# Sparse attention and GELU feed-forward: Winograd's seven products moved from the last batch's input product to unit 1's output product

## The chip, the cores and the metric

The kernel runs on one core of a Trainium2 chip. The time is device microseconds of one execution. Before the change the median of three runs is 221.82 us (221.53 to 222.54). The profiled execution has a span of 220.1 us from its first to its last instruction.

## What is computed

Local attention (window 16) together with block-summary attention, then a two-layer feed-forward with a GELU by sigmoid between the layers. There are 4 batches, 8 heads, 768 positions and a head size of 64, so 3072 tokens of width 512; the hidden width is 2048.

```python
k_sum = k.reshape(B, H, nb, block, D).max(axis=3)       # block = 32, nb = 24
v_sum = v.reshape(B, H, nb, block, D).mean(axis=3)
scores_l = scale * np.matmul(q, k.transpose(0, 1, 3, 2))
scores_s = scale * np.einsum('bhsd,bhnd->bhsn', q, k_sum) + np.log(block)
scores_l_m = np.where(np.abs(pos[:, None] - pos[None, :]) < window, scores_l, -1e9)
a = softmax(np.concatenate([scores_l_m, scores_s], axis=-1))
x = np.matmul(a, np.concatenate([v, v_sum], axis=2))    # to tokens x 512
h = x @ w_in                                            # input product, 512 -> 2048
g = h * (1.0 / (1.0 + np.exp(-1.702 * h)))
out = g @ w_out                                         # output product, 2048 -> 512
```

## The kernel before, in words

Work goes by *units*: a unit is half a batch, 384 tokens (`HALF`), so there are units 0 to 7. For each unit the attention output is turned into `xT` (features on partitions, in two tiles of f16 per unit parity). The input product makes `gT` of 16 tiles of 128 hidden features, the *ff tiles*: each is four matmuls of 384 columns into a PSUM bank (`ph`), and ScalarE (ACT) writes the GELU of it to `gT`. The output product takes 128 tokens at a time, an *output tile*; a unit has three. Plainly done (`ff_out`, line 788) an output tile is 16 matmuls of 512 columns into one bank (`po`), in four parts of four.

Units 2 to 7 form their output tiles in pairs by Winograd's form of Strassen's method (class `Pair`): the product of two output tiles is cut into quarters, and seven products of half size, `p1` to `p7`, each of eight matmuls of 256 columns, give all four quarters of both tiles. The sums of the left factors are made on VectorE (DVE) by `sums`, those of the weights once by `w_sums`; between products parts of the result are copied out of PSUM by ACT (`held`) or added by DVE.

Every operation goes through a helper that records it (`_Ordered`, line 28), so the order on each engine is the order in which the Python code calls, and nearly all instructions have line 28 in the profile. Groups are told apart by the names of their tiles.

The stages that the change touches:

- Unit 1's output product is the loop at the end of `for u in range(2)` (line 1067 on). It has 12 slots (three tiles by four parts). After each slot `beside` puts in work for batch 1's attention, by the table `plan1` (line 1038): `t` turns a pair of heads of q on TensorE (PE) and copies it, `s` and `S` are `scores` (12 matmuls for a half of a pair of heads, an exponential on ACT, a multiplication with the mask on DVE), `v` is `values` (24 matmuls, then a reciprocal and a multiplication on DVE for each of two pairs), `x` turns the result into `xT`. Two pools of PSUM serve all this: `pmm`, four tiles of one bank, and `psb`, two tiles of two banks each. Scores and turned q use `psb`; in this stage `values` uses `pmm`, two tiles at a time. `w_sums(3)` comes after slot 2, and the transposes of batch 2's keys by DMA (`xk`, on the SP queue) after slot 3.
- The units 2 to 5 run through a common loop (line 1176): `ff_in` for each ff tile of one unit, then of the next, with other work put between. After it come the three pairs' 21 products in the order of line 1110.
- The last batch (units 6 and 7) takes another way, `ff_in_pairs` (line 704). Eight ff tiles of unit 6 are made plainly. Then DVE forms the first sums for the pairs of output tiles (`early`) and four sums `xsum` of the two units' `xT`. After that, for four pairs of ff tiles of both units together, seven products of two matmuls each (`A`, `Bp`, `C`, `Dp`) stand in place of eight; unit 7's eight plain ff tiles (`one(u + 1, ...)`) are put between. The sums `wsum` of the input weights are made on DVE in the batch before (`win_weights`, line 691). Between the products DVE moves a partial result from one PSUM tile to another (`px_in`, `pw_in`) or adds a held one (`m`, `c`), and ACT copies or does the GELU.

The order inside a pair of ff tiles is this:

```python
def A(i):
    prod(x, wt[0, 0], b11, i, True)
    dve.tensor_copy(out=y, in_=x)
    prod(v, ws[2], t[2], i, True)
    copy(act, hold[i], v)
def Bp(i):
    prod(x, ws[1], t[1], i)
    dve.tensor_add(v, x, hold[i])
    prod(y, wt[0, 1], b21, i)
    gelu(u, f0(i), y)
```

Of the kernel before, what the change touches and what calls it, by code (L numbers as in the profile page):

```python
# [9 lines left out]
F32 = mybir.dt.float32  # L10
# [25 lines left out]
def kernel(  # L36
# [648 lines left out]
            for nt in range(N0):  # L685
                act.activation(out=gT[0][:, nt, :], in_=ph0[nt], func=ACT.Gelu_apprx_sigmoid)

    WI = 4
    wt = {}

    def win_weights(i0, i1):

        if i0 == 0:
            w = w_in_sb.rearrange("p k (i e c) -> p e k i c", e=2, c=128)[:, :, :, NI - WI:]
            wt.update({(e, h): w[:, e, 2 * h:2 * h + 2] for e in range(2) for h in range(2)})
            wt["s"] = stage.tile([128, 4, 2, WI, 128], F16, name="wsum", tag="kf")
        o, i = [wt["s"][:, n, :, i0:i1] for n in range(4)], slice(i0, i1)
        a11, a12, a21, a22 = (wt[e, h][:, :, i] for e in range(2) for h in range(2))
        dve.tensor_add(o[0], a21, a22)
        dve.tensor_sub(o[1], o[0], a11)  # L700
        dve.tensor_sub(o[2], a11, a21)
        dve.tensor_sub(o[3], a12, o[1])

    def ff_in_pairs(u, early):

        (b11, b21), (b12, b22) = xTT
        xs = castp2.tile([128, 4, 2, HALF], F16, name="xsum", tag="kb")
        t = [xs[:, n] for n in range(4)]
        big = [psb.tile([128, 1024], F32, name="pw_in", tag="big") for _ in range(2)]
        mm = [pmm.tile([128, 512], F32, name="px_in", tag="mm") for _ in range(4)]  # L710
        X = [big[0][:, 0:HALF], big[1][:, 0:HALF], mm[0][:, 0:HALF]]
        V = [b[:, 512:512 + HALF] for b in big]
        Y = [m[:, 0:HALF] for m in mm[1:3]]
        L = mm[3][:, 0:HALF]

        def gelu(w, f, src):
            act.activation(out=gT[w % 2][:, f, :], in_=src, func=ACT.Gelu_apprx_sigmoid)

        def one(w, f, ps):
            for ko in range(KO):  # L720
                pe.matmul(out=ps, lhsT=w_in_sb[:, ko, f * 128:(f + 1) * 128], rhs=xT[w % 2][ko],
                          start=(ko == 0), stop=(ko == KO - 1))
            gelu(w, f, ps)

        def prod(ps, a, b, i, first=False):
            for k in range(2):
                pe.matmul(out=ps, lhsT=a[:, k, i], rhs=b[:, k], start=(first and k == 0),
                          stop=(k == 1), skip_group_check=True)

        ws = [wt["s"][:, n] for n in range(4)]  # L730
        hold = {}

        def A(i):
            x, v, y = X[i % 3], V[i % 2], Y[i % 2]
            prod(x, wt[0, 0], b11, i, True)
            dve.tensor_copy(out=y, in_=x)
            prod(v, ws[2], t[2], i, True)
            hold[i] = attp.tile([128, HALF], F32, name="m7", tag="x2")
            copy(act, hold[i], v)

        def Bp(i):
            x, v, y = X[i % 3], V[i % 2], Y[i % 2]
            prod(x, ws[1], t[1], i)
            dve.tensor_add(v, x, hold[i])
            prod(y, wt[0, 1], b21, i)
            gelu(u, f0(i), y)

        def C(i):
            x, v = X[i % 3], V[i % 2]
            prod(x, ws[0], t[0], i)  # L750
            c = attp.tile([128, HALF], F32, name="c22", tag="a_sb")
            dve.tensor_add(c, x, hold[i])
            prod(v, wt[1, 1], t[3], i)
            gelu(u, f0(i) + 1, v)
            gelu(u + 1, f0(i) + 1, c)

        def Dp(i):
            x = X[i % 3]
            prod(x, ws[3], b22, i)
            gelu(u + 1, f0(i), x)  # L760

        def f0(i):
            return 2 * (NI - WI + i)

        free = [X[0], X[1], X[2], V[0], V[1], Y[0], Y[1], L]
        for f in range(2 * (NI - WI)):
            one(u, f, free[f % 8])
        early()
        for n, (x, y) in ((2, (b22, b12)), (0, (b12, b11)), (1, (b22, t[0])), (3, (b21, t[1]))):
            dve.tensor_sub(t[n], x, y)  # L770
        rest = list(range(2 * (NI - WI)))
        for i in range(WI + 1):
            if i < WI:
                A(i)
            if i:
                C(i - 1)
            one(u + 1, rest.pop(0), L)
            if i < WI:
                Bp(i)
            if i:  # L780
                Dp(i - 1)
            if i < WI - 1:
                one(u + 1, rest.pop(0), L)
        assert not rest

    po_now = {}

    def ff_out(u, ms, part):
# [38 lines left out]
    def bank(name):  # L827
        return pmm.tile([128, d_model], F32, name=name, tag="mm")
# [6 lines left out]
    class Pair:  # L835
# [51 lines left out]
            self.w = bank("pw")  # L887
            product(self.w, self.a21, ts["t3"], True)

        def p2(self):  # L890
            y = bank("py")
            product(y, self.a12, ts["b21"], True)
            dve.tensor_add(self.osb(0)[:, 0:DH], y[:, 0:DH], self.t1)
            self.store(0, 0, False)

        def p4(self):
# [133 lines left out]
    for p in range(NP):  # L1030
# [5 lines left out]


    plan1 = {0: ["t0"], 1: ["t1"], 2: ["s0", "s1"], 4: ["t2"], 5: ["t3"],
             6: ["v0", "s2", "s3"], 8: ["x0"], 9: ["v1", "S0", "S1"], 11: ["x1", "S2", "S3"]}

    plan0 = {-1: ["q0", "q1", "q2", "q3", "s0", "s1"], 3: ["v0", "s2"], 5: ["x0", "s3"], 7: ["v1"], 9: ["x1"]}

# [2 lines left out]
    def beside(u, slot):  # L1045
        b, half = u // 2, u % 2
        for what in (plan0 if u == 1 else plan1).get(slot, ()):
            i = int(what[1])
            if what[0] == "t":
                tq1(i, dve if i % 2 else act)  # L1050
            elif what[0] == "q":
                q_turn(i, 1)
                q_copy(i, dve, 1)
            elif what[0] == "s":
                scores(b, half, i)
                if half and i == NP - 1:
                    gelu_soon()
            elif what[0] == "S":
                scores(b, 1, i)
                if i == NP - 1:  # L1060
                    gelu_soon()
            elif what[0] == "v":
                values(b, half, i, u == 1)
            else:
                tx(i, half)

    for u in range(2):
        todo = {}
        if u == 0:
            for p in range(NP):  # L1070
                todo.setdefault(12 + p // 2, []).append(lambda p=p: cast_q(dve, p, 1))
        else:
            def value_rows():
                vsum(1, range(NJ))
                block_sums()
                halo_dmas(w51, 0)
                sum_dmas(w51, 0)
                load_vc(2)
                load_qc(2)

            todo = {0: [lambda: tk(0, 1)], 3: [lambda: tk(1, 1)], 5: [lambda: v_odd(1)],
                    6: [lambda: tk(2, 1)], 9: [value_rows], 11: [lambda: tk(3, 1)]}
            ff_in(u, range(3))
        for nt in range(0 if u else N0, NT):
            if u == 0 or nt > 2:
                ff_in(u, (nt,))
            for f in todo.get(nt, ()):
                f()
        exp_soon()
        if u == 0:  # L1090
            beside(1, -1)
            load_qc(1)
            load_kc(2)
            busy(6)
        order = [(ms, part) for ms in range(JH) for part in range(4)]
        if u == 0:

            order = [(ms, part) for part in range(4) for ms in range(JH)]
        for i, (ms, part) in enumerate(order):
            ff_out(u, ms, part)  # L1100
            beside(u + 1, i)
            if u == 0 and i in (4, 7, 10):
                w_sums(i // 3 - 1)
            if u == 1 and i == 2:
                w_sums(3)
            if u == 1 and i == 3:
                for g in range(2):
                    xk(g, 2)

    order = ["a7", "a2", "a6", "b1", "a5", "b7", "a3", "a4", "b6", "b2", "b5",  # L1110
             "c1", "b3", "c7", "c6", "c2", "c5", "b4", "c3", "c4"]
# [16 lines left out]
    for b in range(1, B):  # L1128
# [17 lines left out]
        if more:  # L1146
# [21 lines left out]
            when = 7 if b == 1 else 14  # L1168
            first.setdefault(when, []).append(lambda: [xq(g, n) for g in range(2)])
            first.setdefault(9 if b == 1 else 15, []).append(bring)  # L1170
        if b == B - 2:
            for n0 in range(WI):
                first.setdefault(n0, []).append(lambda n0=n0: win_weights(n0, n0 + 1))
        if not more:
            ff_in_pairs(u, lambda: pairs["a"].sums(0, NI - WI))
        for w, todo in ((u, first), (u + 1, second)) if more else ():
            ff_in(w, range(3))
            for nt in range(NT):
                if nt > 2:
                    ff_in(w, (nt,))  # L1180
                for f in todo.get(nt, ()):
                    f()
        pairs["a"].p1(act)
        if more:
            exp_soon()
        if more:
            for m in "bc":
                pairs[m].sums(NI - 1, NI)
        else:
            pairs["a"].sums(NI - WI, NI)  # L1190
            for m in "bc":
                pairs[m].sums(0, NI)
        for what in order:
            getattr(pairs[what[0]], "p" + what[1])()
            if more:
# [32 lines left out]
```

## Time and profile before

| what | value |
|---|---|
| median of three runs | 221.82 us |
| profiled execution, its own time | 221.82 us |
| its span | 220.1 us |
| mean granted clock of TensorE | 0.974 |
| PE busy | 204.5 us, 93% |
| DVE busy | 145.8 us, 66% |
| ACT busy | 123.2 us, 56% |
| POOL busy | 94.6 us, 43% |

The page's times are from the span's start. The busy lines say how long an engine had an instruction in flight; the chain of work that ended last says which instruction each next one had to wait for, followed back from the end. In that chain PE has 69% of the span. PEclk is the share of TensorE's clock that was granted. Matmuls overlap, so the mean duration of one (326 ns for 384 columns) is longer than the time until the next one: in the chain of waits, where the pieces join end to end, 64 such matmuls take 10.53 us.

### The profile page before, as it was taken

How to read it: one execution, taken by the hardware profiler on the slowest of the kernel's cores; microseconds unless marked ns; L12 is line 12 of the kernel's file. 1: busy time of each engine (PE TensorE's matmuls, PEld its weight loads, DVE VectorE, ACT ScalarE, POOL GpSimd, SP SyncE). 2: the span in 40 equal slices, each digit the busy share in tenths (PEclk: the TensorE clock that was granted, in tenths of full speed). 3: DMA queues.
4: the chain of work that ended last, by engine and by line, in shares of the span. 5: the costliest groups of instructions: out<-in, count | busy, mean ns of one | idle time of the engine just before them, and what ended most of it. 6: DMA issues, size and time to landing. Idle time of an engine off the chain costs nothing.

```text
span 220.1 us, 5530 instructions
## 1 busy us (share of the span) xinstructions
PE 204.5 (93%) x2185; PEld 138.2 (63%) x2185; DVE 145.8 (66%) x417; ACT 123.2 (56%) x232; POOL 94.6 (43%) x173
## 2 busy tenths in 40 slices
PE   7869999999799999999999999999999747899994
PEld 2747565556365665667888755678887423558883
DVE  6696936687956769945777862899677143349532
ACT  2773777256475597778334676774437613783220
POOL 7879989799979800609993011020000000000000
PEclk9996999999999999999999999999999967999998
DMA  6999999999999999999999999950433300000223
GB/s 159 297 171 205 268 220 215 157 155 236 153 160 138 160 128 213 155 123 74 121 194 145 167 216 160 107 104 3 131 86 105 112 0 0 0 4 0 95 74 119
DMA packets 96610, 29.34 MB, mean 133 GB/s; under 512 B 84480, under 2 KB 93600, under 8 KB 96584
## 3 DMA queue, kind: packets, MB, share of 16 engines
q0 software_dynamic: 67920, 14.88, 75.9%
q1 hardware_dynamic: 28664, 14.11, 33.0%
q8 instruction: 17, 0.28, 0.5%
q14 instruction: 9, 0.07, 0.1%
HBM read 27.26 MB, written 6.29 MB: 152 GB/s over the span
## 4 chain that ended last, share of the span: by engine, by line
PE 69%; POOL 12%; DMA 7%; DVE 7%; SPq 2%; issue 2%; ACT 0%; DVEq 0%; POOLq 0%
PE ph L28 20%; PE px L28 14%; PE pw L28 8%; PE px_in L28 5%; PE pw_in L28 5%; PE po L28 5%; PE py L28 4%; DMA kb<-in_k_dram 3%; PE ps_s L28 3%; PE ps_av L28 3%; POOL mk L28 2%; POOL kb L28 2%; POOL qb L28 2%; DMA qf<-in_q_dram 2%; DMA qb<-in_q_dram 2%; SPq L28 2%
## 5 line engine op out<-in xcount | busy, mean ns | idle before, releaser
L28 PEld LDWEIGHTS <-w_in_sb 128*128 128x128 f16 x472 | 46.0, 99 | 32.9 <-issue 4.5
L28 PE MATMUL ph<-xT,w_in_sb 128*128 128x384 f16 x384 | 65.0, 326 | 0.0
L28 ACT ACTIVATE gT<-ph 128x384 f16<-128x384 f32 x96 | 45.6, 490 | 21.0 <-PE ph L28 20.8
L28 PEld LDWEIGHTS <-gT 128*128 128x128 f16 x384 | 35.6, 98 | 12.4
L28 ACT ACTIVATE a_sb<-ps_s 128x768 bf16<-128x768 f32 x28 | 21.2, 806 | 11.4 <-PE ps_s L28 11.4
L28 PE MATMUL po<-w_out_sb,gT 128*128 128x512 f16 x96 | 23.1, 380 | 0.0
L28 PEld LDWEIGHTS <-ss 128*128 128x128 f16 x216 | 21.0, 98 | 2.5
L28 DVE TENSOR_TENSOR a_sb<-a_sb,mk 128x768 bf16<-128x768 bf16 x28 | 15.5, 556 | 8.6 <-ACT a_sb L28 7.1
L28 ACT ACTIVATE t<-px 128x256 f32<-128x256 f32 x21 | 8.1, 384 | 20.0 <-PE px L28 20.0
L28 POOL DMA_DIRECT2D vw<-vw x12 | 6.6, 578 | 28.2 <-DVE vw L28 24.3
L28 PE MATMUL pw<-tb,gT 128*128 128x256 f16 x144 | 18.7, 273 | 0.0
L28 PE MATMUL px<-ta,ss 128*128 128x256 f16 x144 | 18.7, 273 | 0.0
L28 DVE TENSOR_TENSOR x<-ps_av,rc 128x384 f16<-128x384 f32 x28 | 15.6, 558 | 1.0
L28 POOL DMA_DIRECT2D vw<-in_v_dram x18 | 15.9, 936 | 0.2 <-issue 0.2
L28 DVE TENSOR_REDUCE ks<-kx 128x24 bf16<-128x768 bf16 x12 | 11.3, 943 | 6.0 <-DMA kx<-kb 6.0
L28 DVE TENSOR_TENSOR ss<-gT 128x512 f16<-128x512 f16 (+3 forms) x18 | 7.5, 418 | 9.9 <-ACT gT L28 9.9
L28 POOL DMA_DIRECT2D kb<-in_k_dram x16 | 13.2, 858 | 1.6 <-DMA w_out_sb<-in_moe_w_out_dram 1.2
L28 POOL DMA_DIRECT2D qb<-in_q_dram x16 | 13.3, 932 | 1.3 <-DMA vw<-in_v_dram 1.3
L28 ACT ACT_TABLE_LOAD x10 | 12.8, 1283 | 1.0 <-PEq L1212 0.8
L28 PE MATMUL px_in<-xT,w_in_sb 128*128 128x384 f16 x58 | 13.2, 360 | 0.0
L28 DVE TENSOR_TENSOR osb<-pw,t 128x256 f32<-128x256 f32 x18 | 7.6, 422 | 8.0 <-PE pw L28 4.8
L28 DVE RECIPROCAL rc<-ps_av 128x6 f32<-128x6 f32 x32 | 6.0, 188 | 7.1 <-PE ps_av L28 6.8
(126 smaller groups left out, 309.6 us busy)
## 6 DMA issues: line engine op xcount, KB each, us to landing
out_dram<-osb SPq DMA_DIRECT2D x18, 256.0 KB, 4.8
vw<-in_v_dram POOLq DMA_DIRECT2D x18, 128.0 KB, 5.5
w_in_sb<-in_moe_w_in_dram POOLq DMA_DIRECT2D x4, 512.0 KB, 8.6
w_out_sb<-in_moe_w_out_dram POOLq DMA_DIRECT2D x4, 512.0 KB, 16.0
kf<-in_k_dram SPq DMA_DIRECT2D x8, 192.0 KB, 4.2
kb<-in_k_dram POOLq DMA_DIRECT2D x16, 96.0 KB, 4.7
qb<-in_q_dram POOLq DMA_DIRECT2D x16, 96.0 KB, 7.0
out_dram<-osb SPq DMA_DIRECT2D x12, 128.0 KB, 1.7
```

The source lines that it names most:

```text
L28: r = f(*a, **kw)
```

## The change

Two edits. The first takes `win_weights` and `ff_in_pairs` out, and the last batch's units 6 and 7 go through the common loop of the other units. The sums of the three pairs are then placed as in batches 1 and 2.

The second replaces unit 1's twelve slots. Output tiles 0 and 1 become a `Pair`, tile 2 stays plain, and its four parts stand between the seven products. `p2` is split, so that the addition and the store of its result come later (`c11`). `w_sums(3)` is called ahead of the slots. In `plan1` `x0` goes from slot 8 to 7 and `v1`, `S0`, `S1` go from slot 9 to 8. `values` takes one `psb` tile for both of its pairs of heads, in place of two `pmm` tiles.

```diff
-        def p2(self):
-            y = bank("py")
-            product(y, self.a12, ts["b21"], True)
-            dve.tensor_add(self.osb(0)[:, 0:DH], y[:, 0:DH], self.t1)
+        def p2(self, early=False):
+            self.y = bank("py")
+            product(self.y, self.a12, ts["b21"], True)
+            if not early:
+                self.c11()
+
+        def c11(self):
+            dve.tensor_add(self.osb(0)[:, 0:DH], self.y[:, 0:DH], self.t1)
             self.store(0, 0, False)
...
-             6: ["v0", "s2", "s3"], 8: ["x0"], 9: ["v1", "S0", "S1"], 11: ["x1", "S2", "S3"]}
+             6: ["v0", "s2", "s3"], 7: ["x0"], 8: ["v1", "S0", "S1"], 11: ["x1", "S2", "S3"]}
...
-                values(b, half, i, u == 1)
+                values(b, half, i, True)
...
-        order = [(ms, part) for ms in range(JH) for part in range(4)]
         if u == 0:
-
-            order = [(ms, part) for part in range(4) for ms in range(JH)]
-        for i, (ms, part) in enumerate(order):
-            ff_out(u, ms, part)
-            beside(u + 1, i)
-            if u == 0 and i in (4, 7, 10):
-                w_sums(i // 3 - 1)
-            if u == 1 and i == 2:
-                w_sums(3)
-            if u == 1 and i == 3:
-                for g in range(2):
-                    xk(g, 2)
+            for i in range(12):
+                ff_out(0, i % JH, i // JH)
+                beside(1, i)
+                if i in (4, 7, 10):
+                    w_sums(i // 3 - 1)
+
+    ss = stage.tile([128, 2, NI, 128], F16, name="ss", tag="vf")
+    pair = Pair((1, 0), (1, 1), ss)
+    w_sums(3)
+    for i, step in enumerate(("p2", "p1", 0, 1, 2, "p7", "p6", "p5", None, "p3", "p4", 3)):
+        if step == "p2":
+            pair.p2(True)
+        elif step == "p1":
+            pair.p1(act)
+        elif step in (0, 1, 2, 3):
+            ff_out(1, 2, step)
+        elif step:
+            getattr(pair, step)()
+        beside(2, i)
+        if i == 1:
+            pair.sums(0, NI)
+            pair.c11()
+        if i == 3:
+            for g in range(2):
+                xk(g, 2)
...
-        if b == B - 2:
-            for n0 in range(WI):
-                first.setdefault(n0, []).append(lambda n0=n0: win_weights(n0, n0 + 1))
-        if not more:
-            ff_in_pairs(u, lambda: pairs["a"].sums(0, NI - WI))
-        for w, todo in ((u, first), (u + 1, second)) if more else ():
+        for w, todo in ((u, first), (u + 1, second)):
             ff_in(w, range(3))
...
-        if more:
-            for m in "bc":
-                pairs[m].sums(NI - 1, NI)
-        else:
-            pairs["a"].sums(NI - WI, NI)
-            for m in "bc":
-                pairs[m].sums(0, NI)
+        for m in "bc":
+            pairs[m].sums(NI - 1, NI)
```

## The prediction

> **What bounds the kernel now.** I read the chain of waits in order of time first, since it says which engine sets the end in each stage; then the busy time and granted clock by stretches; then the order of time on single engines where the chain has gaps. From 60.35 us on the chain is nearly all PE: unit 1's output product runs from 63.45 to 78.96, and from there every stage is PE work end to end, but for the last batch's input product.
>
> ```profile
> 63.45 0.86 PE po L28 x4
> 64.31 0.34 PE ps_t L28 x6
> ...
> 66.70 0.46 PE ps_s L28 x24
> 67.16 1.83 PE po L28 x8
> ...
> 101.41 0.87 PE px L28 x8
> 102.28 0.87 PE pw L28 x8
> ...
> 124.53 10.53 PE ph L28 x64
> 135.07 0.45 PE ps_vs L28 x24
> 135.52 10.51 PE ph L28 x64
> ```
>
> These are start, duration and piece. A part of `ff_out` costs 0.86 us, one of the seven half-size products 0.87 us, a pair of score pieces 0.46 us. Batch 2's input product, of both units and with nothing in its way, is 10.53 + 10.51 = 21.04 us.
>
> The same product in the last batch takes 29.34 us, from 169.15 to 198.49, with fewer matmuls. The busy times by stretches (stretch, length, then busy time of PE, PEld, DVE, ACT, POOL, the granted clock, DMA) say why:
>
> ```profile
> 124.53:146.02 21.49, 21.49 (x155) 12.83 (x153) 14.94 (x52) 14.77 (x31) 3.40 (x6) 1.00 1.22 159
> 169.15:198.49 29.34, 23.20 (x123) 12.49 (x121) 11.20 (x22) 15.73 (x35) 0.00 (x0) 0.88 0.11 32
> ...
> 174.49:178.91 4.42, 0.32 (x3) 0.09 (x1) 3.71 (x8) 0.49 (x1) 0.00 (x0) 0.88 0.00 0
> 178.91:181.00 2.09, 2.09 (x7) 1.01 (x7) 0.00 (x0) 0.49 (x1) 0.00 (x0) 0.50 0.00 0
> 181.00:183.55 2.55, 2.55 (x9) 1.22 (x8) 0.57 (x1) 0.98 (x2) 0.00 (x0) 0.50 0.00 0
> ...
> 188.42:190.69 2.27, 1.62 (x10) 0.88 (x9) 1.15 (x3) 1.56 (x4) 0.00 (x0) 1.00 0.00 0
> ```
>
> PE stands still for over 4 us, the clock falls to half, and stays there until about 183.6. What it waits for is in PE's own order of time, the idle time and its releaser in brackets:
>
> ```profile
> 178.91 0.80 PE L28 MATMUL pw_in<-xsum,wsum 128*128 128x384 f16 x2 [4.10 <-DVE px_in L28]
> ...
> 190.69 0.48 PE L28 MATMUL pw_in<-xsum,w_in_sb 128*128 128x384 f16 x2 [0.65 <-DVE c L28]
> ```
>
> **Edit 1, the last batch.** Removed: 4 pairs x 7 products x 2 = 56 matmuls; added: 4 x 16 = 64. So PE has 128 matmuls of 384 columns in place of 120, 8 more at 0.164 us (10.53 / 64), 1.3 us more work. Removed with them is all that made 120 matmuls (120 x 0.164 = 19.7 us) last 29.34, that is 9.6 us: the wait of 4.42 us for DVE (three sums for the output pairs, four `xsum`, then the copy to `px_in`, one after the other from 175.04 to 178.86); the half clock after it (16 matmuls from 178.91 to 184.2 take 5.3 us instead of 2.6, so 2.7); and the later waits for one DVE operation on a PSUM tile, 0.65 us each where the chain shows them in full, the remaining 2.5 us together. The common loop waits for nothing of the kind: batch 2 does it in 21.04 us, its GELU takes 0.49 us of ACT for every 0.65 us of PE, and the sums for the output pairs lie beside it on DVE. The last batch has less beside it (no key halos, no `ps_vs`). I take 29.34 - 21.04 = **8.3 us off**. For the range: if only the 4.42 us wait and its clock went, it would be 4.42 + 2.7 - 1.3 = 5.8 us; more than 8.3 is not there, as PE would have to beat batch 2.
>
> The 16 `wsum` operations on DVE (0.28 us each, 4.6 us from 125.3) go too, at no gain: PE ran end to end there. The tail is the same 21 products, 198.49 to the end, 21.6 us, without a stall then or now: its first product needs `gT` of unit 6 only, made 10 us earlier, and the 6 + 3 sums that DVE did beside it are mostly done before.
>
> **Edit 2, unit 1, work.** Removed: 8 parts at 0.86 = 6.88 us. Added: 7 products at 0.87 = 6.09 us. **0.8 us off**, as all of this stage is PE (15.51 busy of 15.51). The first product needs the last GELU of the odd ff tiles in its eighth matmul only, at 63.45 + 7 x 0.109 = 64.2, and ACT ends it at 63.97.
>
> **Edit 2, the DVE and ACT side.** DVE gets three sums of 0.69 us, one subtraction of 0.69 and three additions of 0.42 more, 4.0 us on 9.65 busy of 15.51. In order: `w_sums(3)` from 63.6 to 65.2, the copy of turned q to 66.6, the sums to 68.55. `p7`, which needs them, is PE's next but three: 63.45 + 2 x (0.87 + 0.34) + 0.86 + 0.46 + 1.83 + 0.34 = 69.4. So they are hidden by 0.8 us; without this cover `p7` would be late by what exceeds it. ACT swaps two copies of 0.60 for four of 0.38, 0.3 us more, on 9.73 of 15.51, hidden by the same idle time.
>
> **Edit 2, new waits.** `values` now takes a `psb` tile, of which there are two. In the changed program, as built, `v0` and `v1` have one of the two and `s2`, `s3`, `S0`, `S1` all have the other. So `s3` must wait until the exponential of `s2` has read it, and `S1` for that of `S0`. Before, each found the other tile free. The price comes from the pair s0, s1:
>
> ```profile
> 66.64 0.52 PE L28 MATMUL ps_s<-qT,kx 64*128 64x64 bf16 x24
> ...
> 67.03 1.51 ACT L28 ACTIVATE a_sb<-ps_s 128x768 bf16<-128x768 f32 x2 [0.84 <-PE ps_s L28]
> ...
> 67.87 1.26 DVE L28 TENSOR_TENSOR a_sb<-a_sb,mk 128x768 bf16<-128x768 bf16 x2 [1.43 <-ACT a_sb L28]
> ```
>
> By the chain the first 12 of the 24 end at 66.70 + 0.23 = 66.93; ACT starts 0.10 later, runs 0.81 (mean of the group `a_sb<-ps_s`), and a released PE starts 0.05 later (178.86 to 178.91 above). That is **0.96 us, twice**, with PE idle, and behind the waiting matmul stands all PE work. The lower bound is nothing; the upper takes ACT late by one copy of 0.38, 1.34 us each. There is a third: `v1` needs the mask product of `s3`, which comes 0.10 + 0.81 + 0.03 + 0.59 (half of two in 1.18) + 0.05 = 1.58 us after `s3`; between them lie `p5` (0.98 with its start after scores), `x0` (0.34) and half of `v1` (0.25), 1.57 in all, where two parts and more lay before. I take nothing; up to 0.7 if DVE is late by an addition and the reciprocal. Sum of edit 2: -0.8 + 1.92 = **1.1 us on**, between -0.8 and +2.6.
>
> A rule speaks against these short waits. The Trainium skill, TensorE: Matmul & The Clock Gate, "A second HAM failure mode: psum-queue depth-cycling", says that frequent small idles between matmul groups, from cycling through PSUM, can make the clock go to and fro between half and full. By it the 6 us of PE work from the first wait to the next stage could take 12, and the time would be about 220.6 us. This trace has the same kind of wait, 0.65 us before 190.69, and the granted clock around it is 1.00; only the 4.42 us wait was followed by 0.50. I go by the row, 214.6 us.
>
> **SP and POOL queues.** `xk`'s four transposes stood in the SP queue behind the store of unit 1's first tile, which waited for `osb` until 69.02, and began at 69.62. Now only unit 0's stores are ahead, so they begin when batch 2's keys have landed, near 56.2 + 5.5 = 61.7 us. They then run beside the block rows for `v0`, the transfers `vw<-vs`, issued at 62.37 and 63.46, which land after 3.6 us, at 67.1. `v0` comes at 71.4, so 4.3 us of delay cost nothing. If they took as long as the slowest transpose (10.0 us), they would land at 73.5 and `v0` wait 2.0 us. I take 0. Unit 1's stores end at about 80, ahead of `dx`, which follows in the queue at 83 as before.
>
> **The sum.** 220.1 - 8.3 + 1.1 = 212.9 us of span; the profiled execution's time is 1.72 us over its span and equals the median, so 214.6 us.
>
> **Rivals.** *The new waits do not show* (0.12): ACT or order hides them; then edit 2 gives -0.8 and the time is 212.7. For it: ACT has 5.8 us idle in the stage. Against it: nothing is placed between `s2` and `s3`. *Unit 1 costs more* (0.13): `v0` waits 2.0 us for its rows, or ACT and DVE are late everywhere; 216.1 to 216.6; one spell of half clock alone (2.7) would give 217.3. For it: DMA engines are full at 67 to 79. Against it: 4.3 us of slack. *The last batch recovers less* (0.05): the low clock there has another cause and stays; 21.04 / 0.85 = 24.8, 3.7 less to gain, or 218.3 us. Against it: batch 2 ran at 1.00. *Slower* (0.04): the block rows queue behind all four transposes. These took 9.53 us to issue and up to 10.0 to land, so 61.7 + 19.5 = 81.2, and `v0` would wait 9.8 us, with the half clock 2.7 more: 227.1 us. It makes the kernel slower from a wait of 5.6 us (214.6 + 5.6 + 2.7 = 222.9), that is rows landing after 77.0. Against it: every `vw` transfer in that stage landed within 6.4 us.
>
> **How the numbers follow.** The forecast, 213.8 to 215.8, has 0.65, and 0.01 is left for mishaps that add up to no change. The range goes down to 212.5 for the first rival and up to 217.4 for the second. This kernel's measurements can tell 0.5%, 1.1 us, from no change. Faster 0.95, same 0.01, slower 0.04.
>
> **What would show it.** The changed profile should have 128 `ph` matmuls of the last batch in 21 us with a clock of 1.00 and no `px_in`; PE waits of about 1 us for ACT `a_sb` ahead of `s3` and `S1`; and unit 2's first `ph` at about 80.1 instead of 78.96. A PE wait for `vw` or for `ss`, a clock under 1.00 in unit 1, or a last batch over 22 us would prove a step wrong.

## The result, and the profile after

| | median | runs |
|---|---|---|
| before | 221.58 us | 220.94 to 222.54, six runs |
| changed | 214.95 us | 213.57 to 215.95 in five runs, 223.28 in a sixth |

The ratio is 0.9685 (95% interval 0.9638 to 0.9733): the changed kernel is faster by 3.2%, some 7 us. Some executions are disturbed, here the one of 223.28 us; the ratios, here and below, leave such executions out, the medians and ranges of the experiments do not. The profiled execution of the changed kernel took 214.01 us, with a span of 212.3.

The busy times by stretches of the changed kernel, for unit 1's output product and for the last batch's input product (columns as before: stretch, length, PE, PEld, DVE, ACT, POOL, clock, DMA):

```profile
61.83:79.02 17.19, 15.36 (x253) 11.60 (x252) 13.31 (x33) 10.39 (x17) 11.06 (x14) 1.00 1.97 130
169.93:190.73 20.80, 20.80 (x130) 12.58 (x129) 5.85 (x14) 14.76 (x31) 0.00 (x0) 1.00 0.15 45
```

The second line is the gain: 20.80 us, all of it busy, clock 1.00, where 29.34 us stood with a clock of 0.88. The first line is the price: 17.19 us with 15.36 busy, where the kernel before had 15.51, all busy:

```profile
63.45:78.96 15.51, 15.51 (x229) 8.96 (x228) 9.65 (x24) 9.73 (x15) 12.50 (x15) 1.00 1.72 139
```

The chain of waits of the changed kernel shows what fills the rest of unit 1:

```profile
61.83 0.87 PE py L28 x8
...
68.94 0.87 PE px L28 x8
...
70.03 0.54 PE ps_av L28 x23
70.57 0.30 PE ps_s L28 x12
...
70.89 0.82 ACT a_sb L28
...
71.75 0.35 PE ps_s L28 x12
72.11 0.98 PE px L28 x8
...
73.98 0.30 PE ps_s L28 x12
...
74.30 0.82 ACT a_sb L28
...
75.16 0.35 PE ps_s L28 x12
75.52 0.98 PE px L28 x8
```

Twice ACT's exponential stands between two halves of scores, and the chain goes through it. From `s2` at 70.57 to the product at 72.11 are 1.54 us; the pair took 0.46 before. So each wait costs 1.08 us. PE's waits over the whole execution, by what they waited for (us in total, times, longest):

```profile
PE ps_s L28 <- ACT a_sb L28: 1.8, 2, 0.9
...
PE ph L28 <- DMA xT<-x: 0.7, 1, 0.7
```

The second line is new too, and lies in batch 2. No full wait for the rows of `v0` shows in this execution, but `v0`'s 24 matmuls stretch from 69.81 to 70.57, 0.76 us in place of 0.50. The two transfers of the rows were issued at 62.37 and 63.56 (62.37 and 63.46 before), but landed only at about 69.7 and 69.9, just when `v0` began. The queues show what had changed: the order of time of the SP queue (start, duration, operation) and the rows' transfers (number, size of each, median us from issue to landing). The kernel before:

```profile
69.62 9.53 SPq L28 DMA_TRANSPOSE kx<-kq  x4
```

```profile
vw<-vs POOLq DMA_DIRECT2D x2, 148.5 KB, 3.6
```

The changed kernel:

```profile
61.22 8.75 SPq L28 DMA_TRANSPOSE kx<-kq  x4
```

```profile
vw<-vs POOLq DMA_DIRECT2D x2, 148.5 KB, 6.8
```

The transposes of batch 2's keys began 8.4 us earlier by the clock of the span and now run beside the rows `vw<-vs`, which landed 6.8 us after their issue in place of 3.6. An experiment below moves these transposes alone.

The span's account: last batch 8.54 off; unit 1 1.68 on (17.19 - 15.51); the new wait for `xT` 0.7 on; and unit 1 began at 61.83 instead of 63.45, 1.6 us earlier. That last part is not the change: in the profiled execution before, PE stood 1.59 us for DVE `ks` at 60.35, ahead of all that was edited. In no other profile is this wait longer than 0.2 us, and `before_filled` below, which has the same code up to there, began unit 1 at 61.7. -8.5 + 1.7 + 0.7 - 1.6 = -7.7, and the spans differ by 7.8. Without the earlier start the change is worth 6.2 us in these two profiles.

### The profile page after: what moved, and what is told of

Read it like the earlier page. It is cut to its first block, busy times and chain, and to the rows that moved or that the text cites. A ratio compares the mean times of both kernels' runs of the same rounds, so it can differ in the third digit from the quotient of the medians.

```text
span 212.3 us, 5559 instructions
## 1 busy us (share of the span) xinstructions
PE 201.9 (95%) x2217; PEld 140.9 (66%) x2217; DVE 136.7 (64%) x401; ACT 122.7 (58%) x230; POOL 94.8 (45%) x173
## 2 busy tenths in 40 slices
DMA packets 96610, 29.34 MB, mean 138 GB/s; under 512 B 84480, under 2 KB 93600, under 8 KB 96584
## 4 chain that ended last, share of the span: by engine, by line
PE 84%; DMA 10%; DVE 1%; POOL 1%; ACT 1%; SPq 1%; issue 0%
PE ph L28 39%; PE px L28 16%; PE pw L28 7%; PE po L28 7%; PE ps_av L28 4%; DMA xT<-x 4%; PE py L28 4%; DMA vb<-in_v_dram 4%; PE ps_s L28 3%; DMA kf<-in_k_dram 2%; PE ps_t L28 1%; PE ps_x L28 1%; POOL vb L28 1%; ACT a_sb L28 1%; DVE qT L28 1%; PE ps_vs L28 1%
## 5 line engine op out<-in xcount | busy, mean ns | idle before, releaser
L28 PE MATMUL ph<-xT,w_in_sb 128*128 128x384 f16 x512 | 86.0, 326 | 0.7 <-DMA xT<-x 0.7
L28 ACT ACTIVATE gT<-ph 128x384 f16<-128x384 f32 x128 | 60.9, 490 | 26.2 <-PE ph L28 26.0
L28 PEld LDWEIGHTS <-w_in_sb 128*128 128x128 f16 x512 | 49.4, 98 | 33.0 <-issue 1.2
L28 PEld LDWEIGHTS <-ss 128*128 128x128 f16 x240 | 23.1, 98 | 2.9
L28 DVE TENSOR_TENSOR ss<-gT 128x512 f16<-128x512 f16 (+3 forms) x22 | 8.7, 394 | 19.6 <-ACT gT L28 19.6
L28 PE MATMUL pw<-tb,gT 128*128 128x256 f16 x160 | 20.8, 273 | 0.0
L28 PE MATMUL px<-ta,ss 128*128 128x256 f16 x160 | 20.8, 273 | 0.0
L28 PE MATMUL po<-w_out_sb,gT 128*128 128x512 f16 x64 | 15.2, 380 | 0.0
L28 PE MATMUL ps_s<-qT,kx 64*128 64x64 bf16 (+3 forms) x400 | 10.0, 192 | 2.8 <-ACT a_sb L28 1.8
L28 PEld LDWEIGHTS <-kx 64*128 64x128 bf16 x400 | 7.7, 96 | 6.5 <-issue 5.9
```

What stands on the lines that cost most here:

```text
L28: r = f(*a, **kw)
```

## The experiments

Ratios are to the kernel before, run on the same chip as the kernel in question (its medians there: 220.8, 220.4, 220.5 and 220.9 us); in brackets stand 95% intervals.

**The two edits apart.** The first kernel, `last_plain`, is the kernel before with edit 1 only (`win_weights` and `ff_in_pairs` out, the common loop for the last batch); the second, `unit1_pair`, has edit 2 only.

> Edit 1 alone: the last batch goes through the common loop, unit 1 stays as before. My theory says that the whole gain is here: the last batch's input product falls from 29.3 to about 20.8 us, clock 1.00, and the time is 221.6 - 8.4 = 213.2 us, under the changed kernel's 214.95. Rival: unit 1's pair brings part of the gain (it has 0.8 us less PE work); then this alone gives more than 214.95.

> Edit 2 alone: unit 1 by the seven products, the last batch as before. My theory: slower by what the changed profile shows, unit 1 17.2 us instead of 15.5, that is 221.6 + 1.7 = 223.3 us, with two PE waits for the exponential of 0.9 us each. Rival, that the pair pays as its 0.8 us less PE work says: 220.8 us.

Measured: 212.79 us (211.90 to 213.58), ratio 0.9641 [0.9602, 0.9681]; and 224.15 us, ratio 1.0116 [1.0063, 1.0168]. By the ratios edit 1 alone gives 7.9 us and all of the gain; edit 2 alone costs 2.6 us (1.4 to 3.7). With both, the ratio is 0.9685, so beside edit 1 the second edit costs about 1 us (0.9685 / 0.9641 = 1.0046, across chips), though the two intervals overlap. The chain of waits of the kernel with edit 1 alone has a wait of its own:

```profile
79.37 2.59 PE ph L28 x16
81.96 8.17 DMA xT<-x
...
90.18 1.95 PE ph L28 x11
```

Unit 1 is 1.6 us shorter there, and PE stands 0.7 us at 90.18 for unit 3's `xT`. What a slower unit 1 loses, this wait can give back in part. But the changed kernel's wait of 0.7 us in batch 2 is not in this kernel, so by the two profiles the waits cancel and do not explain why the cost is nearer to 1 us than to 1.7.

**The half clock.** `before_filled` is the kernel before, with four plain ff tiles of unit 7 ahead of the sums that PE waited for; they no longer stand between the half-size products. The matmuls are the same.

```diff
+        rest = list(range(2 * (NI - WI)))
+        for n in range(4):
+            one(u + 1, rest.pop(0), free[n])
         early()
...
```

> The kernel before, with four of unit 7's plain ff tiles moved ahead of the first sums, so that PE has 2.6 us more to do while DVE makes them. My theory of the last batch: the wait of 4.1 us falls to about 1.7, which is too short to halve the clock, so 2.4 + 2.7 = 5.1 us are won; the DVE waits further on have less work beside them and give 0.5 to 1.5 us back: 216.5 to 217.5 us, clock 1.00 throughout. Rival, that the half clock comes from the small products themselves: the clock stays at 0.50 for a while and the time is 218.5 us or more.

Measured: 218.07 us, ratio 0.9897 [0.9857, 0.9936]. The same stretches of that kernel:

```profile
169.60:195.10 25.50, 21.33 (x122) 11.51 (x121) 10.93 (x23) 15.93 (x35) 0.00 (x0) 1.00 0.13 38
174.49:178.91 4.42, 3.61 (x22) 1.96 (x20) 3.23 (x8) 2.86 (x6) 0.00 (x0) 1.00 0.00 0
```

With the long wait covered the clock stays at 1.00, so the half clock came from that wait and not from the half-size products. The stage is 3.8 us shorter in the profile (29.34 - 25.5), but the ratio gives only 2.3 us, less than expected. Two things on record go that way: this profiled execution has 1.9 us of PE waits for `xT` that the one of the kernel before lacks, and that one had a mean granted clock of 0.974, where most executions of the kernel before on record had 0.984 to 0.992, so most lose less to a low clock. Most of the rest, 25.5 against 20.8, is waits for single operations: of DVE (0.77 for `px_in`, then 0.65 to 0.66 for `px_in` or `c`, and 0.32) and of ACT's GELU (0.58 and 0.31). No run removes these without the pairs.

**Edit 2's waits.** `plain_values_psb` is edit 1 alone, with the one line `values(b, half, i, True)`: unit 1's output product stays plain, but `values` takes its tile from `psb`. `scores_apart` is the changed kernel with the scores set so that no two exponentials follow each other.

```diff
-             6: ["v0", "s2", "s3"], 7: ["x0"], 8: ["v1", "S0", "S1"], 11: ["x1", "S2", "S3"]}
+             6: ["v0", "s2"], 7: ["s3", "x0"], 9: ["v1", "S0"], 10: ["S1"], 11: ["x1", "S2", "S3"]}
```

> Edit 1, and in unit 1 only the values put into the pool of two tiles; products and table as before. My theory: the waits come from the pool and not from the products, so the two PE waits of 0.9 us are here too and the time is that of edit 1 alone plus about 2.1 us, 215.3 us. Rival, that the products' copies on ACT and sums on DVE make the waits: no wait, 213.2 us.

> The changed kernel with a product between the two score pieces that share a PSUM tile (s3 after p5, v1 and S0 after p3, S1 after p4). My theory: p5 and p4 (0.87 us each) cover the exponential (0.9 us), both PE waits go, unit 1 falls from 17.2 to about 15.1 us and the time to 214.95 - 2.0 = 213.0 us. Rival, that the stage is bound by the chain of exponential, mask and values whatever the order: a wait of the same size shows ahead of v1 or x1, and the time stays at 214.9 us.

Measured: 214.21 us (0.9693 [0.965, 0.9736]) and 215.94 us (0.9725 [0.9662, 0.9787]). In the first, PE's order of time has the two waits, without any of the seven products (idle time before, and its releaser, in brackets):

```profile
70.45 0.35 PE L28 MATMUL ps_s<-qT,kx 64*128 64x64 bf16 x12 [0.90 <-ACT a_sb L28]
...
75.52 0.35 PE L28 MATMUL ps_s<-qT,kx 64*128 64x64 bf16 x12 [0.90 <-ACT a_sb L28]
```

Unit 1 takes 17.67 us instead of 15.55, 2.1 more; the kernel loses 1.4 us by the medians (1.1 by the ratios, whose intervals overlap), and its profile lacks the wait of 0.7 us for `xT`. So the waits are the pool's, not the products'. The second kernel missed both expectations: the exponential's waits are gone, and it is no faster, because `v0`'s rows now decide. Its order of time on PE, and the stretches after it:

```profile
69.49 0.19 PE L28 MATMUL ps_av<-vw,a_sb 128*64 128x65 bf16 x1 [0.53 <-ACT t L28]
71.41 0.54 PE L28 MATMUL ps_av<-vw,a_sb 128*64 128x65 bf16 x23 [1.73 <-DMA vw<-vs]
```

```profile
69.01:71.41 2.40, 0.19 (x1) 0.14 (x2) 0.68 (x1) 0.37 (x1) 2.40 (x4) 1.00 1.80 180
...
73.00:74.57 1.57, 1.57 (x21) 1.11 (x20) 1.28 (x3) 1.19 (x3) 0.84 (x2) 0.50 1.96 153
74.57:76.28 1.71, 1.71 (x12) 0.96 (x10) 1.03 (x2) 0.10 (x1) 0.53 (x1) 0.50 2.73 145
```

PE stood 1.73 us for `vw<-vs`, and the clock was at half from 73.0 to 76.3. Unit 1 took 19.1 us in this execution.

**The keys' place in the SP queue.** `plain_xk_early` is edit 1 alone with the keys' transposes issued at slot 0 instead of 3, ahead of unit 1's first store. `tile2_first` is the changed kernel with the four parts of the plain tile together, and the transposes at slot 5, behind that tile's store. The edit of `tile2_first` against the changed kernel:

```diff
-    for i, step in enumerate(("p2", "p1", 0, 1, 2, "p7", "p6", "p5", None, "p3", "p4", 3)):
+    for i, step in enumerate(("p2", "p1", 0, 1, 2, 3, "p7", "p6", "p5", None, "p3", "p4")):
...
-        if i == 3:
+        if i == 5:
```

> Edit 1 alone, and the four key transposes of batch 2 put one place ahead in the SP queue, before unit 1's first store in place of behind it. Nothing else moves. My theory for what unit 1 costs beyond the two waits for the exponential: the transposes now begin near 61 us in place of 67 and delay the block rows of v0, which land after 6 to 13 us in place of 4 to 5; PE waits 0.5 to 5 us for DMA vw ahead of v0, and the time is 213.5 to 217 us against 212.8 of edit 1 alone, with a wider spread. Rival, that v0's wait belongs to the seven products (an earlier v0, a busier DVE): no wait for vw, 212.8 us.

> The changed kernel, with the plain tile's last part moved from the last slot to the fourth of its kind, so that its store stands ahead of the key transposes in the SP queue again, as before the change. My theory: the transposes begin near 68 us, v0 no longer waits for its rows; the two waits for the exponential (0.9 us each) stay. Time 212.8 (edit 1 alone) - 0.8 (PE work) + 2.1 = 214.1 us with a spread under 2 us. Rival, that the rows are late for another reason: v0 still waits, 215 us or more.

Measured: 213.33 us (212.04 to 216.90), ratio 0.9662 [0.9613, 0.9711]; and 213.42 us (212.49 to 215.40), ratio 0.9695 [0.9649, 0.9742]. In the first, the rows of `v0` are late in a unit 1 that has no other edit. Edit 1 alone, with the keys behind the store:

```profile
67.06 8.23 SPq L28 DMA_TRANSPOSE kx<-kq  x4
```

```profile
vw<-vs POOLq DMA_DIRECT2D x2, 148.5 KB, 4.8
```

The same with the keys early, and what PE then waits for:

```profile
61.27 10.10 SPq L28 DMA_TRANSPOSE kx<-kq  x4
```

```profile
vw<-vs POOLq DMA_DIRECT2D x2, 148.5 KB, 7.4
```

```profile
PE ps_av L28 <- DMA vw<-vs: 0.6, 1, 0.6
```

So the early keys make the rows late. What that costs the whole kernel is not clear of noise (0.9662 and 0.9641, the intervals overlap). In the second the rows land after 3.5 us and `v0` takes 0.50 us again; the exponential's waits stay, and unit 1 takes 17.17 us. By the ratio it is no faster than the changed kernel (0.9695 and 0.9685, the intervals overlap). `tile2_first_apart` then has both: the plain tile first and the scores apart.

> As tile2_first, and a product between the score pieces that share a PSUM tile. My theory: neither wait is left, and only the saved PE work is seen: 212.8 - 0.8 = 212.0 us, unit 1 in about 14.9 us. It would be the fastest of all. Rival, that the stage then meets the next limit (px copied out by ACT between p6 and p5, the norm ahead of x1): 212.8 us or more.

Measured: 215.87 us (213.20 to 220.81), ratio 0.9747 [0.9687, 0.9806], a miss: 212.0 us was expected. The profile is of an execution of 216.93 us, about 1 us over the median. PE's waits there:

```profile
PE ph L28 <- DMA xT<-x: 4.7, 2, 2.7
```

Unit 1 ran from 60.90 to 76.10, 15.2 us, with no wait for the exponential and 0.15 us idle; what it gained was lost, and more, at unit 3's first `ph`, which waits for the transposes of its `xT`. They land 9.8 to 11.5 us after their issue, against 4.4 to 5.1 in the kernel before. How much of these 4.7 us the shorter executions have, no profile shows.

**The transposes replaced by plain copies.** Is it the transposes that hold up the other transfers, or just the bytes and the time at which they are asked for? In four kernels the 22 transposes by DMA (keys, q and `x` of the later batches) become plain copies of the same bytes into the same tiles (the keys' four as eight). These kernels leave out the turning, so their attention output is not the right one; the rest is in place. The copy of `x`, as one of the three:

```diff
...
-        sp.dma_start(out=xTT[m][g].rearrange("p i (j c) -> p (i j) c", c=128),
-                     in_=x2[g].rearrange("p i j h d -> p (i j h d)"), transpose=True)
+        sp.dma_start(out=xTT[m][g].rearrange("p i s -> p (i s)"),
+                     in_=x2[g].rearrange("p i j h d -> p (i j h d)"))
```

> Edit 1 alone, with the 22 transposes by DMA (kx, qT, xT of the later batches) replaced by plain copies of the same bytes to the same tiles: the keys, q and x of those units are not turned, so the output differs; all else is in place. It is the base for the two kernels beside it. Expected 209 to 212: the 0.7 us wait for unit 3's xT goes, and the attention outputs of batches 2 and 3 have shorter waits at most. Rival: the transposes do not slow the other transfers, and it stays at 212.8.

> The changed kernel with the same plain copies in place of the transposes by DMA (the same part is not turned). Theory: what delayed v0's rows were the transposes that run beside them; then vw<-vs lands after 3 to 4 us, v0 takes 0.50 us, and edit 2 costs what is left of it, two waits of 1.07 less 0.8 us of work: 0.4 to 1.4 us over the kernel with edit 1 alone and the same copies. Rival: the rows are late for another reason (the POOL queue, the loads of v and q), and the distance stays at 2 us or more.

> The changed kernel with the scores set apart (no two exponentials in a row) and the same plain copies in place of the transposes by DMA. Theory: with neither the exponential's wait nor late rows, the seven products' work is all that is left of edit 2: 0.8 us under the kernel with edit 1 alone and the same copies, unit 1's output product in 14.7 to 15.0 us at a clock of 1.00. Rival: an earlier unit 2 gives nothing, since what it needs next (unit 3's xT, batch 2's keys) does not come earlier; then it is the same within 0.3 us, with a wait of PE in unit 2 or 3 for DMA.

> The kernel with the plain tile first and the scores apart (unit 1 without waits, but 4.7 us of waits for unit 3's xT), with the same plain copies in place of the 22 transposes by DMA (the same part is not turned). Batch 2's keys again go behind the plain tile's store, so the rows of v should land after about 4 us as in the kernel with edit 1 alone and these copies (211.5 us). Theory: what ate the 0.8 us of the seven products there was xT's transposes meeting the other transfers; with plain copies PE waits for neither rows nor xT, unit 1's output product takes 14.7 to 15.0 us and the time is 210.7, 0.8 under that kernel's ratio to before (0.955 instead of 0.959). Rival: unit 3's start or batch 2's keys are late with any form of transfer; then PE waits over 1 us there and the time is 211.5 or more.

| kernel, with the copies | median us | ratio to before | unit 1, us | rows `vw<-vs` land after, us |
|---|---|---|---|---|
| edit 1 alone | 211.48 | 0.9589 [0.9555, 0.9623] | 15.51 | 3.9 |
| changed | 215.15 | 0.9745 [0.9691, 0.9799] | 18.58 | 6.4 |
| changed, scores apart | 212.11 | 0.9611 [0.9571, 0.9651] | 16.87 | 6.7 |
| changed, plain tile first, scores apart | 211.05 | 0.9567 [0.9516, 0.9618] | 15.28 | 3.9 |

The first met its expectation: its profile has no wait for unit 3's `xT`. The theory of the second fell: no transpose is left, and the rows are late all the same. Its edit 2 costs 3.4 us beside the first kernel (0.9745 and 0.9589, the intervals apart), over the 2 us that its rival named. Its keys' copies begin at 59.90 us, and PE waits:

```profile
69.58 0.19 PE L28 MATMUL ps_av<-vw,a_sb 128*64 128x65 bf16 x1 [0.97 <-DMA vw<-vs]
70.12 0.54 PE L28 MATMUL ps_av<-vw,a_sb 128*64 128x65 bf16 x23 [0.35 <-DMA vw<-vs]
```

So what makes the rows late is when the keys' transfers are asked for, not their form. The kernels with the keys at 67.0 to 69.6 us have the rows after 3.5 to 4.8 us (eight profiles, transposes and copies); those with the keys at 59.9 to 61.9 have them after 6.1 to 7.4 us (five). The profile of edit 2 alone, of an execution of 228.08 us, has the keys at 62.9 and the rows after 9.2.

The last kernel has neither wait, and PE stands only 0.2 us for `xT`, where its twin with transposes stood 4.7 us; whether the form of `xT`'s own transfers or the lighter traffic did that is not separated. The third, `apart_copies`, missed for the same reason as `scores_apart`: 1.5 us of waits for the rows. Set against the first, the last is the only test of what the seven products are worth without the waits: unit 1 takes 15.28 us against 15.51, all busy in both. That is 0.23 us, not 0.8, and the two ratios' intervals overlap. Its chain of waits shows where the rest went:

```profile
69.79 0.98 PE px L28 x8
...
71.05 0.44 PE ps_x L28 x6
71.49 0.87 PE px L28 x8
72.37 0.64 PE ps_av L28 x24
...
73.29 0.98 PE px L28 x8
...
74.55 0.98 PE pw L28 x8
```

A product after scores or values takes 0.98 instead of 0.87 (after `ps_t` or `ps_x` it stays at 0.87). By the chain's pieces: 12 parts took 10.65 us; seven products and four parts take 6.42 + 3.55, 0.68 off. Two pairs of scores in halves take 0.28 four times instead of 0.46 twice, 0.20 on; `v1` 0.64 instead of 0.50; one `x` 0.44 instead of 0.34. Sum: 0.24 off.

## Why the prediction was right

The time, 214.6 us, is 0.35 from the median, by the mechanism that it named. Point by point:

- *Edit 1, 8.3 us off*: 8.5 in the profile, 7.9 by edit 1's own ratio. The clock was 1.00 all through that stage, and the kernel with the wait filled showed that the wait made the half clock.
- *Edit 2, work 0.8 us off*: 0.79 by the chain (9.86 against 10.65). It holds only as long as the pieces around it keep their forms; with the scores apart, 0.23 us of unit 1's time was left.
- *New waits, 0.96 us twice*: both there, at the place foretold and for ACT `a_sb`; mis-sized, since each cost 1.08. The wait itself is 0.90, and the two halves of the scores take 0.30 and 0.35 us, where the sum had 0.23 each.
- *DVE and ACT hidden*: no wait for `ss` showed.
- *SP and POOL queues, taken as 0*: this is the step that was too small. It gave the rows 4.3 us of slack and took the transposes as no burden. In the profiled execution the slack is used up: the rows landed some 2.7 us later than before, and `v0` came 1.6 us earlier (69.8 and not 71.4), since unit 1 began earlier. The slack had been read from a profile with the wait of 1.59 us for `ks` in it. In the five profiles with early keys counted above the rows land after 6.1 to 7.4 us, 2.5 to 3.8 more than the 3.6 of before. In the profiled execution `v0` took 0.26 us more and `v1` 0.06; in the others of these kernels PE waits 0.6 to 1.7 us for the rows. The rival *unit 1 costs more*, by a wait of `v0` for its rows, appears in these in part. The rival *slower*, with the rows queued behind all four transposes until 81.2 us, does not: in the five profiles they landed by 71.3, and plain copies delay them as much. Edit 2's 2.6 us alone need no further cause, since 1.7 lies within their interval.
- *Sum of edit 2, 1.1 us on*: in unit 1 it is -0.79 + 2.16 + 0.32 = 1.69 on. Over the whole kernel it is about 1.0 by the ratios, which the noise does not part from 1.7.
- *The total*: part of the agreement is luck. The forecast was 8.3 - 1.1 = 7.2 us off; the profiles have 8.5 - 1.7 - 0.7 = 6.2, and the earlier start of unit 1, which nobody foretold, brings 1.6 more. The ratio gives 7.0.
- *The rule on short waits*: two waits of 0.90 us each left the clock at 1.00, as the row had it.

Unit 2's first `ph` came at 79.02, not 80.1; 1.6 us of that is the earlier start, and with it removed unit 1 is 0.6 longer than foretold.

The shortest kernel with nothing left out is, by the medians, edit 1 alone, 212.79 us. Not measured: moving the loads of batch 2's q behind unit 3's `xT`, which might let an earlier unit 2 pay.

## What to carry to other kernels

Fewer products are worth less than their matmuls when they need PSUM tiles or DVE results in a row: in the last batch they saved 1.3 us of work and brought 9.6 us of waits and half clock, and in unit 1 less than a third of 0.8 us was left in the best arrangement. When an edit takes a store out of its place in a queue, whatever stood behind it starts earlier, and its cost must be looked for in the transfers that it now runs beside. Before shortening a stage, look at what the next stage waits for: if that is a transfer, the saving can come back as a wait.

## What was not expected of the hardware

The length of idle time that halves the clock was shorter than thought. Over the runs: 0.90 us, 1.12 us with 0.19 busy, 1.59 us with 0.12 busy, and 1.91 us without a matmul (`tile2_first_apart`, from 88.15) were followed by a granted clock of 1.00. In `scores_apart` 2.40 us with 0.19 busy (no single wait over 1.73) was followed by 0.50 for 3.3 us, which began only 1.6 us after PE had resumed. In `tile2_first_apart` 2.74 us without a matmul, from 91.21, was followed by 0.50 at once, for 3.4 us. The 4.42 us with 0.32 busy in the kernel before were followed by 0.50 as well. The Trainium skill, TensorE: Matmul & The Clock Gate, "What's actually happening", lets the clock fall after at least one idle window of about 3.4 us, with windows that do not start with the kernel's work. The 4.42 us wait agrees; the stretches of 2.40 and 2.74 us are shorter than such a window and the clock was halved after them all the same, so here the measurement decides.

The same skill, Advanced Engine Details and Errata, "X-Bar Transpose (TRN2)", says that transposes by DMA are as fast as regular ones. For the keys nothing speaks against it: with edit 1 alone, issuing them took 8.23 us as four transposes and 12.68 as eight copies in pieces of 128 bytes, and with early keys the rows were as late beside the one (6.1 to 7.4 us) as beside the other (6.4 and 6.7). For batch 2's q, whose copies are in pieces of 3072 bytes, the runs do not agree with it. With edit 1 alone, as transposes and as copies:

```profile
qT<-kq SPq DMA_TRANSPOSE x2, 9.7
```

```profile
qT<-kq SPq DMA_DIRECT2D x2, 384.0 KB, 5.2
```

Over the kernels the transposes landed after 6.3 to 12.9 us and the copies after 4.2 to 5.2. The traffic beside them differed as well, so how much of this is the turning itself is not shown.
